# A different order of the first loads, and of the first matmuls, in a gated S5 and MLP kernel

## The chip, the core and the metric

The kernel runs on one core of a Trainium2 chip. The metric is the device time of one execution in microseconds (us). Before the change three runs took 214.64, 214.77 and 215.53 us, so the time before is 214.77 us, their median.

## What is computed

For 2048 tokens x of width 640 the kernel computes two branches and mixes them with a gate of one number per token:

```python
g = sigmoid((x * gate_w).sum(-1, keepdims=True))
# branch A: a diagonal complex recurrence of 640 states, and a skip
Bu = einsum("bld,pd->blp", x, B_bar)
h  = Lam_bar * h + Bu[:, t, :]            # for t in range(2048)
a  = 2.0 * einsum("blp,dp->bld", hseq, Cmat).real + x * Dskip
# branch B: a two-layer perceptron with 1728 hidden units
b  = gelu(x @ w1 + b1) @ w2 + b2
out = g * a + (1 - g) * b
```

All inputs and the output are bf16.

## The kernel before

**Tiles.** The tokens are cut into four chunks of 512, and a chunk into four token tiles of 128. The width 640 is five blocks of 128, counted by `kd`. A matmul needs x with its width on the partitions, so each chunk has a turned copy `xT[c]` of 128 partitions x 5 blocks x 512 tokens. The hidden width 1728 is thirteen blocks of 128 and a rest of 64, counted by `kf`. The first six blocks of w1 (768 columns) lie in five tiles `w1a[kd]`, one for each row strip of w1; in this text a strip is the 128 rows of one `kd`. The next four blocks are `w1b[kd]`, the rest is `w1c`.

**Main order.** After the start the kernel goes through the chunks: `ff1` (x times w1, with GELU on ScalarE, lines 274 to 321), `ssm` (x times B on TensorE, then the recurrence on VectorE), `fin_b` (times w2) and `fin_a` (times C, and the final mix). The order on TensorE, VectorE and ScalarE is the order in which the program is written (line 195 sets a manual schedule); the function `later` and its relatives place VectorE's work by estimated times. DMAs are issued by three engines: SyncE (SP), ScalarE (ACT) and GpSimd (POOL), each in program order.

**The first loads.** For chunk 0 the turned copy is made in two ways. Width blocks 0 and 1 of each token tile are loaded as they are (`load_x0`, lines 134 to 142, 64 KB for a tile) and turned by TensorE against an identity (`turn`, line 239); the result in PSUM is copied to `xT[0]` by VectorE for block 0 and by ScalarE for block 1 (`turned`, line 243). Width blocks 2 to 4 come by a transposing DMA, one for each half of the chunk (`load_turned`, lines 149 to 153). Lines 137 to 143 issue, on SyncE: token tile 0, strip 0 of `w1a`, token tile 3, strip 2; on ScalarE: token tile 1, strip 1, token tile 2. After that SyncE issues the two transposes and strips 4 and 3. A strip of `w1a` is 192 KB in rows of 1536 B. Behind its three loads ScalarE has a table load for its functions and a first `Exp` (line 147).

**The first matmuls.** Lines 236 and 237 fill the wait for the first data with nine matmuls on constants, whose results are not used. `turn_first(a, ...)` (line 251) turns both blocks of token tile `a`. Lines 357 to 369 then write the order out by hand: `part(kd, a)` is six matmuls of 128 columns, one for each of six `kf`, of strip `kd` with token tile `a`; `strip(kd, t0, t1, ...)` is the same with the tokens from t0 to t1. The six `kf` add up in six PSUM banks (`banks`), and with `pA` and one more bank for the turning all eight banks of PSUM are taken. After `part(1, 3)` come strip 2 in two halves (it needs the transposing DMAs), strip 4 and strip 3 (lines 376 to 393).

**A second chain in the start.** The matmul at line 370 turns a tile of small parameters. From it VectorE makes the arguments of the sine tables (lines 371 to 383), ScalarE loads the sine table and computes both tables (lines 382 and 384), then loads the GELU table and begins the GELUs of chunk 0 (line 282). Later ScalarE writes a bias into one bank (line 292), which the 20 matmuls of line 299 need.

Of the kernel before, what the change touches and what calls it, by code (L numbers as in the profile page):

```python
# [16 lines left out]
P = 128  # L17
T = 2048
D = 640
# [8 lines left out]
TPC = CH // P  # L28
H = TPC // 2
HT = H * P  # L30
# [11 lines left out]
def kernel(  # L42
# [19 lines left out]
    nc = tc.nc  # L62
# [12 lines left out]
    def bank(dtype=F32):  # L75
        return ps.tile([P, CH * 4 // (4 if dtype == F32 else 2)], dtype, name="bank")


    cut1 = FA * P
# [4 lines left out]
    w1a = [const.tile([P, cut1], BF16, name=f"w1a_{kd}") for kd in range(KD)]  # L84
# [37 lines left out]
        r0 = c * CH + a0 * P  # L122
        (queue or nc.sync).dma_start(out=xn[c][:, a0:a1, :], in_=x2d[r0:r0 + (a1 - a0) * P, :].rearrange("(a p) d -> p a d", p=P))

    def load_w1a(queue, kd):
        queue.dma_start(out=w1a[kd][:], in_=B_w1[kd * P:(kd + 1) * P, 0:cut1])

    def rows(queue, dst, v):
        queue.dma_start(out=dst, in_=v.rearrange("(j p) -> j p", p=P))
# [1 line left out]
    KA = 2  # L131
    xn[0] = xnp.tile([P, TPC, D], BF16, name="xn")

    def load_x0(queue, a0, a1, d0, d1):
        queue.dma_start(out=xn[0][:, a0:a1, d0:d1], in_=x2d[a0 * P:a1 * P, d0:d1].rearrange("(a p) d -> p a d", p=P))  # L135

    load_x0(nc.sync, 0, 1, 0, KA * P)
    load_x0(nc.scalar, 1, 2, 0, KA * P)
    load_w1a(nc.sync, 0)
    load_w1a(nc.scalar, 1)  # L140
    load_x0(nc.sync, 3, 4, 0, KA * P)
    load_x0(nc.scalar, 2, 3, 0, KA * P)
    load_w1a(nc.sync, 2)
    nc.vector.memset(prmA[:], 0.0)
    nc.vector.memset(prmB[:], 0.0)
    warm = const.tile([P, 1], F32, name="warm")
# [2 lines left out]
    def load_turned(a):  # L149
        nc.sync.dma_start_transpose(out=xT[0][:, KA:KD, a * P:(a + H) * P], in_=x2d[a * P:(a + H) * P, KA * P:D])  # L150

    load_turned(0)
    load_turned(H)
    load_w1a(nc.sync, 4)
    load_w1a(nc.sync, 3)
# [27 lines left out]
        nc.sync.dma_start(out=w2_sb[:, k0:k1, :], in_=B_w2[k0 * P:k1 * P, :].rearrange("(kf p) d -> p kf d", p=P))  # L183
    for h in range(2):
        nc.sync.dma_start(out=w2l[h * F_LAST:(h + 1) * F_LAST, :], in_=B_w2[(KF - 1) * P:F, :])
    load_x0(nc.sync, 0, H, KA * P, D)
    load_x0(nc.sync, H, TPC, KA * P, D)
    nc.sync.dma_start(out=b2bc[:], in_=B_b2.rearrange("(o d) -> o d", o=1).to_broadcast([P, D]))
    nc.sync.dma_start(out=Dbc[:], in_=A_Dskip.rearrange("(o d) -> o d", o=1).to_broadcast([P, D]))
    nc.sync.dma_start_transpose(out=xT[2][:], in_=x2d[2 * CH:3 * CH, :])  # L190
# [42 lines left out]
    nc.vector.tensor_copy(out=tf[:, NQ:NP], in_=tfi[:])  # L233
    ones = lambda n: nc.const_aps.tensor(1.0, [P, n], BF16)
    pA = bank()
    for n in (512, 512, 512, 512, 512, 128, 128, 128, 128):
        nc.tensor.matmul(pA[:, 0:n], lhsT=ones(P), rhs=ones(n), start=True, stop=True)

    def turn(p, col, a, kd):
        nc.tensor.matmul(p[:, col:col + P], lhsT=xn[0][:, a, kd * P:(kd + 1) * P], rhs=ident[:], start=True, stop=True,  # L240
                         skip_group_check=True)

    def turned(engine, p, col, a, k0, k1):
        dst = xT[0][:, k0:k1, a * P:(a + 1) * P]
        src = p[:, col:col + (k1 - k0) * P].rearrange("p (k t) -> p k t", t=P)
        if engine is nc.vector:
            nc.vector.tensor_copy(out=dst, in_=src)
        else:
            nc.scalar.activation(out=dst, in_=src, func=ACT.Identity)

    def turn_first(a, other, t=None):
        t = t or bank()
        turn(t, 0, a, 0)
        turned(nc.vector, t, 0, a, 0, 1)
        turn(other, a * P, a, 1)
        turned(nc.scalar, other, a * P, a, 1, 2)

    turn_first(0, pA)
    def col(name, dtype=F32, n=KS):
        return const.tile([P, n], dtype, name=name)  # L260
# [13 lines left out]
    def ff1_mm(p, c, kf, kd, t0=0, t1=CH, first=None, last=KD - 1):  # L274
        w, f0 = (w1a, 0) if kf < FA else (w1b, FA) if kf < FB else (w1c, FB)
        w = w[kd][:, (kf - f0) * P:(kf - f0 + 1) * P]
        nc.tensor.matmul(p[:, t0:t1], lhsT=w, rhs=xT[c][:, kd, t0:t1],  # L277
                         start=(kd == 0) if first is None else first, stop=(kd == last), skip_group_check=first is not None)
        pe(t1 - t0)
# [51 lines left out]
    def strip(kd, t0, t1, first, f0=0, f1=FA):  # L331
        for kf in range(f0, f1):
            ff1_mm(banks[kf], 0, kf, kd, t0, t1, first, 3)
# [20 lines left out]
    def part(kd, a):  # L354
        strip(kd, a * P, (a + 1) * P, kd == 0)

    turn_first(1, banks[FA - 1], banks[FA - 2])
    for _ in range(3):
        nc.tensor.matmul(banks[0][:, 0:P], lhsT=ones(P), rhs=ones(P), start=True, stop=True, skip_group_check=True)
    part(0, 0)  # L360
    part(0, 1)
    part(1, 0)
    turn_first(2, pA)
    part(1, 1)
    turn_first(3, pA)
    part(0, 2)
    part(1, 2)
# [367 lines left out]
```

## Time and profile before

The profiled execution has a span of 212.8 us, and its run took 214.58 us. TensorE's granted clock has a mean of 0.999 over the span.

| engine | busy us | share of the span | instructions |
|---|---|---|---|
| TensorE matmul (PE) | 208.9 | 98% | 1382 |
| TensorE weight load (PEld) | 125.0 | 59% | 1382 |
| VectorE (DVE) | 183.2 | 86% | 335 |
| ScalarE (ACT) | 102.0 | 48% | 184 |
| GpSimd (POOL) | 62.7 | 29% | 101 |

A row of a timeline gives the start in us, the duration from the first start to the last end, the engine, the line, the operation, what it writes and reads, the shape and the count; in brackets stands the idle time before it and what ended it. "SPq" and "ACTq" are the queues on which SyncE and ScalarE issue DMAs: such a row is the time that the issuing takes, not the transfer. A matmul's duration includes the time that it takes to drain; matmuls overlap, so the distance from start to start (the pitch) tells what one costs. A list of DMA issues gives the line, the queue, the count, the KB of each and the median us from issue to landing.

### The profile page before, as it was taken

What the parts mean: (1) busy time and instruction counts of PE and PEld (TensorE: products, weight loads), DVE (VectorE), ACT (ScalarE), POOL (GpSimd) and SP (SyncE); (2) the same over time, 40 slices, a digit from 0 to 9 for tenths busy, and PEclk for the clock granted to TensorE, in tenths of its full rate; (3) what the DMA queues carried; (4) which work ended last, traced back from release to release, by engine and by line L of the source; (5) the groups of instructions that cost most, each with busy time, mean ns of one, the idle gap of its engine ahead of it and who ended that gap; (6) DMA issues with size and microseconds to landing.
All of it is one profiled execution on the core that took longest, in us unless ns stands there. A gap on an engine that the chain in (4) does not pass through costs nothing.

```text
span 212.8 us, 3603 instructions
## 1 busy us (share of the span) xinstructions
PE 208.9 (98%) x1382; PEld 125.0 (59%) x1382; DVE 183.2 (86%) x335; ACT 102.0 (48%) x184; POOL 62.7 (29%) x101
## 2 busy tenths in 40 slices
PE   7999999999999999999999999999999999999994
PEld 4744444454576544774456777444457587676773
DVE  1589999999989999999999999999999999903153
ACT  3599856675858687103653210456682422205100
POOL 7044079764432462404235503146000000000000
PEclk9999999999999999999999999999999999999999
DMA  6999999995000000051000005100000000100011
GB/s 182 249 221 219 218 212 366 217 217 154 3 0 0 3 0 0 12 186 65 0 0 3 0 17 171 62 0 0 0 5 14 0 3 31 62 34 0 0 63 65
DMA packets 33314, 16.24 MB, mean 76 GB/s; under 512 B 24720, under 2 KB 33296, under 8 KB 33296
## 3 DMA queue, kind: packets, MB, share of 16 engines
q1 hardware_dynamic: 32560, 15.64, 29.7%
q10 hardware_dynamic: 576, 0.36, 0.5%
q8 instruction: 11, 0.18, 0.3%
q14 instruction: 7, 0.06, 0.1%
q0 software_dynamic: 160, 0.01, 0.1%
HBM read 7.48 MB, written 2.62 MB: 47 GB/s over the span
## 4 chain that ended last, share of the span: by engine, by line
PE 97%; DMA 2%; SPq 0%; DVE 0%; issue 0%
PE bank L602 27%; PE bank L277 27%; PE bank L661 20%; PE bank L545 20%; DMA w1a<-in_B_w_dram 2%; PE bank L618 1%; PE bank L299 1%; SPq L135 0%; PE bank L240 0%; DVE ot L666 0%; PE bank L387 0%; PE bank L370 0%
## 5 line engine op out<-in xcount | busy, mean ns | idle before, releaser
L602 PE MATMUL bank<-w_sb,gel 128*128 128x384 bf16 (+1 forms) x416 | 57.9, 299 | 0.0
L602 PEld LDWEIGHTS <-gel 128*128 128x128 bf16 x416 | 40.3, 98 | 17.0 <-issue 0.8
L548 ACT ACTIVATE bu<-bank 128x512 bf16<-128x512 f32 x40 | 23.6, 605 | 37.5 <-PE bank L545 37.5
L282 ACT ACTIVATE gel<-bank,colB 128x512 bf16<-128x512 f32 x52 | 34.0, 695 | 10.8 <-PE bank L277 10.6
L661 PEld LDWEIGHTS <-hs 128*128 128x128 bf16 x330 | 31.7, 98 | 11.6
L509 POOL TENSOR_SCALAR e<-g,cq 128x2 f32<-128x2 bf16 x15 | 18.3, 1222 | 64.3 <-DVE g L502 64.3
L502 DVE TENSOR_TENSOR_SCAN g<-r_c,carry,v 128x512 bf16<-128x512 f32 x30 | 37.2, 1271 | 0.0
L610 ACT ACTIVATE gb<-bank,gcol 128x384 f32<-128x384 f32 (+1 forms) x32 | 15.1, 526 | 33.7 <-PE bank L618 16.8
L277 PE MATMUL bank<-xT,w1a 128*128 128x512 bf16 (+2 forms) x162 | 27.0, 324 | 0.3 <-DMA w1a<-in_B_w_dram 0.3
L661 PE MATMUL bank<-CT_re,hs 128*128 128x320 bf16 (+2 forms) x165 | 27.1, 295 | 0.0
L661 PE MATMUL bank<-CT_im,hs 128*128 128x320 bf16 (+2 forms) x165 | 27.1, 295 | 0.0
L666 DVE SCALAR_TENSOR_TENSOR ot<-bank,gcol,gb 128x320 bf16<-128x320 f32 (+2 forms) x33 | 17.4, 533 | 9.7 <-PE bank L661 9.5
L545 PE MATMUL bank<-xT,BT_re 128*128 128x512 bf16 x100 | 24.8, 379 | 0.0
L545 PE MATMUL bank<-xT,BT_im 128*128 128x512 bf16 x100 | 24.8, 379 | 0.0
L277 PEld LDWEIGHTS <-w1a 128*128 128x128 bf16 x162 | 13.8, 98 | 12.2 <-DMA w1a<-in_B_w_dram 0.6
L576 DVE TENSOR_TENSOR bank<-xn,Dbc 128x320 f32<-128x320 bf16 (+2 forms) x33 | 14.6, 484 | 7.0 <-ACT gb L610 7.0
L277 PE MATMUL bank<-xT,w1b 128*128 128x512 bf16 x80 | 17.9, 379 | 0.0
L545 PEld LDWEIGHTS <-BT_im 128*128 128x128 bf16 x100 | 9.8, 98 | 11.8
L511 POOL TENSOR_TENSOR carry<-e,e 128x1 f32<-128x1 f32 x30 | 15.8, 546 | 1.2
L545 PEld LDWEIGHTS <-BT_re 128*128 128x128 bf16 x100 | 9.7, 98 | 11.0
L483 DVE TENSOR_TENSOR v<-wa,wb 128x512 bf16<-128x512 bf16 x40 | 15.2, 422 | 0.6
L591 ACT ACTIVATE bank<-b2bc 128x384 f32<-128x384 bf16 (+1 forms) x24 | 11.7, 529 | 7.2 <-DVE ot L666 7.2
(110 smaller groups left out, 216.2 us busy)
## 6 DMA issues: line engine op xcount, KB each, us to landing
out_dram<-ot SPq DMA_DIRECT2D x15, 160.0 KB, 1.8
w_sb<-in_B_w_dram SPq DMA_DIRECT2D x2, 640.0 KB, 6.8
xn<-in_A_x_dram SPq DMA_DIRECT2D x2, 640.0 KB, 4.3
w_sb<-in_B_w_dram SPq DMA_DIRECT2D x1, 800.0 KB, 9.6
w1a<-in_B_w_dram SPq DMA_DIRECT2D x4, 192.0 KB, 3.3
w1b<-in_B_w_dram SPq DMA_DIRECT2D x5, 128.0 KB, 3.3
xn<-in_A_x_dram SPq DMA_DIRECT2D x4, 160.0 KB, 3.0
xn<-in_A_x_dram SPq DMA_DIRECT2D x2, 192.0 KB, 8.3
```

The source lines that it names most:

```text
L277: nc.tensor.matmul(p[:, t0:t1], lhsT=w, rhs=xT[c][:, kd, t0:t1], start=(kd == 0) if first is None else first, stop=(kd == last), skip_grou ...
L282: nc.scalar.activation(out=gel[c][:, kf, :], in_=p[:, :], func=ACT.Gelu_apprx_tanh, bias=b1_c[:, kf:kf + 1])
L483: nc.vector.tensor_tensor(out=o, in0=a, in1=b, op=op)
L502: nc.vector.tensor_tensor_scan(s["g"][:, ri, :], r_c[:, ks:ks + 1].to_broadcast([P, CH]), s["v"][:, ri, :], init, ALU.mult, ALU.add)
L509: nc.gpsimd.tensor_scalar(out=t[:], in0=g[:, :, CH - 1], scalar1=f[:, ks:ks + 1], scalar2=None, op0=ALU.mult)
L511: nc.gpsimd.tensor_tensor(out=carry[:, ri, ks:ks + 1], in0=m[0][:, ri:ri + 1], in1=m[1][:, 1 - ri:2 - ri], op=op)
L545: nc.tensor.matmul(p[:], lhsT=BT[ks >= KSA][:, kd, (ks % KSA if ks < KSA else ks - KSA) * P:][:, 0:P], rhs=xT[c][:, kd, :], start=(kd == 0 ...
L548: nc.scalar.activation(out=bu[:, ri, :], in_=p[:], func=ACT.Identity)
L602: nc.tensor.matmul(p[:, col:col + d1 - d0], lhsT=gel[c][:, kf, a * P:(a + 1) * P], rhs=w2_sb[:, kf, d0:d1], start=False, stop=False, skip_ ...
L610: nc.scalar.activation(out=gbs[ti][:, d0:d1], in_=p[:, col:col + d1 - d0], func=ACT.Identity, scale=gcol[:, 1, ti:ti + 1])
L661: nc.tensor.matmul(p[:, 0:d1 - d0], lhsT=hs[c][:, j, lo:lo + P], rhs=CT[:, j % KS, d0:d1], start=False, stop=(j == 2 * KS - 1), skip_group ...
L666: nc.vector.scalar_tensor_tensor(out=ot[:, d0:d1], in0=p[:, 0:d1 - d0], scalar=gcol[:, 0, ti:ti + 1], in1=gbs[ti][:, d0:d1], op0=ALU.mult, ...
```

## The change

The edits, all in the start but for one load:

- ScalarE's queue now issues strip 0 of `w1a` in two halves of 384 columns (96 KB, rows of 768 B): the first half, token tile 1, the second half, token tile 2. That is four DMAs where there were three.
- SyncE's queue issues token tile 0, then strip 1, token tile 3, the first transpose, strip 2, the second transpose, strips 4 and 3.
- A later load on SyncE, width blocks 2 to 4 of token tiles 0 to 3, becomes one DMA in place of two.
- Two of the nine matmuls on constants are left out.
- For token tile 0, block 1 is copied from PSUM by VectorE instead of ScalarE.
- `part(1, 0)` and `part(1, 1)`, which stood around the turning of token tile 2, become one `strip(1, 0, 256)` of six matmuls of 256 columns behind that turning.

```diff
-    def load_w1a(queue, kd):
-        queue.dma_start(out=w1a[kd][:], in_=B_w1[kd * P:(kd + 1) * P, 0:cut1])
+    def load_w1a(queue, kd, f0=0, f1=cut1):
+        queue.dma_start(out=w1a[kd][:, f0:f1], in_=B_w1[kd * P:(kd + 1) * P, f0:f1])
...
     load_x0(nc.sync, 0, 1, 0, KA * P)
+    load_w1a(nc.scalar, 0, 0, cut1 // 2)
+    load_w1a(nc.sync, 1)
     load_x0(nc.scalar, 1, 2, 0, KA * P)
-    load_w1a(nc.sync, 0)
-    load_w1a(nc.scalar, 1)
     load_x0(nc.sync, 3, 4, 0, KA * P)
+    load_w1a(nc.scalar, 0, cut1 // 2)
     load_x0(nc.scalar, 2, 3, 0, KA * P)
-    load_w1a(nc.sync, 2)
...
     load_turned(0)
+    load_w1a(nc.sync, 2)
     load_turned(H)
...
-    load_x0(nc.sync, 0, H, KA * P, D)
-    load_x0(nc.sync, H, TPC, KA * P, D)
+    load_x0(nc.sync, 0, TPC, KA * P, D)
...
-    for n in (512, 512, 512, 512, 512, 128, 128, 128, 128):
+    for n in (512, 512, 512, 512, 512, 128, 128):
...
-        turned(nc.scalar, other, a * P, a, 1, 2)
+        turned(nc.scalar if a else nc.vector, other, a * P, a, 1, 2)
...
     part(0, 0)
     part(0, 1)
-    part(1, 0)
     turn_first(2, pA)
-    part(1, 1)
+    strip(1, 0, HT, False)
     turn_first(3, pA)
```

## The prediction

> **What bounds the kernel now.** I read the busy table first (in the section above): TensorE works 98% of the span. Then the chain of waits in order of time, because only what lies on it can move the end. Its first pieces, with start and duration in us:
>
> ```profile
> 0.72 0.40 SPq L135
> 1.12 0.06 issue
> 1.18 3.30 DMA w1a<-in_B_w_dram
> 4.48 0.05 issue
> 4.52 1.18 PE bank L277 x18
> ```
>
> From 4.52 us to 209.99 us every piece of the chain is TensorE work, so the kernel is one wait for strip 0 of w1, then TensorE without a pause, then a short tail. The change can gain only by starting that work earlier or by taking idle time out of it. So next the timeline of the start:
>
> ```profile
> 3.27 0.63 PE L240 MATMUL bank<-ident,xn 128*128 128x128 bf16 x4
> 3.70 0.49 PE L359 MATMUL bank<-const-bfloat16-1.0 128*128 128x128 bf16 x3
> ...
> 4.52 1.18 PE L277 MATMUL bank<-xT,w1a 128*128 128x128 bf16 x18 [0.34 <-DMA w1a<-in_B_w_dram]
> ...
> 5.54 0.28 PE L240 MATMUL bank<-ident,xn 128*128 128x128 bf16 x2
> ...
> 5.65 0.50 PE L277 MATMUL bank<-xT,w1a 128*128 128x128 bf16 x6
> 5.80 0.29 DVE L247 CAST xT<-bank 128x128 bf16<-128x128 f32 x1 [1.67 <-PE bank L240]
> ...
> 6.14 0.27 PE L240 MATMUL bank<-ident,xn 128*128 128x128 bf16 x2
> ```
>
> Two idle stretches show. The first ends at 4.52 with strip 0. The second is small: the six matmuls from 5.65 have a pitch of (0.50 - 0.22)/5 = 0.056 us (one alone lasts 0.22 in the group's own list), so the last starts at 5.93 and the next could start at 5.99. It starts at 6.14, 0.05 after VectorE's copy of token tile 2 ends (5.80 + 0.29). The turn of tile 3 needs the PSUM bank that this copy empties, so 0.15 us are lost.
>
> When data came is read from the list of DMA issues, asked in narrow windows. The four in flight between 1.4 and 2.0 us:
>
> ```profile
> w1a<-in_B_w_dram ACTq DMA_DIRECT2D x1, 192.0 KB, 3.6
> w1a<-in_B_w_dram SPq DMA_DIRECT2D x1, 192.0 KB, 3.3
> xn<-in_A_x_dram SPq DMA_DIRECT2D x1, 64.0 KB, 3.3
> xn<-in_A_x_dram ACTq DMA_DIRECT2D x1, 64.0 KB, 3.5
> ```
>
> With the issue times of the timeline (1.15, 1.18, 1.64, 1.65) they land at 4.75, 4.48, 4.94 and 5.15. Other windows of the same list give: tiles 0 and 1 at 2.8 and 2.9, strip 2 at 5.8, the transposes at 7.1 and 7.7 (2.59 + 4.5, 3.96 + 3.7), strip 4 at 8.6 (5.28 + 3.3).
>
> Last, the ScalarE rows and the weight load that waits for them:
>
> ```profile
> 12.19 4.73 ACT L282 ACTIVATE gel<-bank,colB 128x512 bf16<-128x512 f32 x8
> ...
> 18.56 0.47 ACT L292 ACTIVATE bank<-b1x 128x260 f32<-128x260 bf16 x1
> 18.87 1.34 ACT L282 ACTIVATE gel<-bank,colB 128x512 bf16<-128x512 f32 x2
> ...
> 19.08 0.66 PEld L299 LDWEIGHTS <-xT 128*128 128x128 bf16 x20 [0.32 <-ACT bank L292]
> ```
>
> ScalarE works without a gap from 10.3 us on, and its row L292 ends at 19.03, just as TensorE needs it (its next matmul starts at 19.09, with no idle time). TensorE can gain over this place only if the ScalarE chain moves too. It does: that chain begins with the matmul L370 at 7.26 (then VectorE, the sine tables, the GELU table load at 10.89), which is in TensorE's order behind the part that moves.
>
> **What the Trainium skill says.** "DMA: Bandwidth & Descriptors", section "Queues, rings and completion order": SP and ACT own one ring each on the same 16 engines, and an engine goes round among the rings. The trace agrees: the two strips, one on each queue, land 0.27 us apart, and the mean DMA share is 1.09 from 3.25 to 4.50 us. So a load that moves to the other queue gains place, not bandwidth. "TensorE: Matmul & The Clock Gate", section "What's actually happening": TensorE starts at half clock and is released after a busy window of about 3.4 us; the window runs free of the kernel. The trace agrees: the turns at 3.27 have a pitch of (0.63 - 0.31)/3 = 0.107 us, the matmuls from 4.52 one of (1.18 - 0.22)/17 = 0.056 us. The release lies between, over 3 us after the first matmul (0.76).
>
> **The change, part by part.**
>
> *Loads.* I put each landing on a curve "KB asked for up to here, time of landing" from the kernel before: 128 KB at 2.9, 512 KB at 4.6 (mean of 4.48 and 4.75), 640 KB at 5.05, 832 KB at 5.8. This assumes that the two rings share bytes evenly. After the change ScalarE's ring holds 96 (strip 0a), 64 (tile 1), 96 (strip 0b), 64 (tile 2), and SyncE's 64 (tile 0), 192 (strip 1), 64 (tile 3), then the first transpose. A load ends when its own ring has given its KB and the other as many. Strip 0a: 192 KB at most, 3.2. Tile 1: 320 KB, 3.75. Strip 0b and strip 1: 512 KB, 4.6. Tiles 2 and 3: 640 KB, 5.05 to 5.15. No row shows these landings in the new order; I keep 4.8 and 5.6 as the ends for tile 2 (the first two rivals) and take 5.15.
>
> *Start.* Two matmuls on constants fewer: 0.21 us at a pitch of 0.107, hidden before and after by the wait for loads. Tile 0 is turned at 3.06, tile 1 at 3.8 when it lands. VectorE now makes three copies where it made two (0.29 each; tile 0's lie in the wait), and the third follows the turn by 0.36 (3.27 to 3.63 before): 4.16 to 4.45. ScalarE issues a fourth DMA (0.45), so table load (1.28) and Exp (0.20) end near 4.1 instead of 3.63; its one copy (tile 1) runs from 4.27 to 4.55, hidden by strip 0b. The first three matmuls of strip 0 can run near 4.3 with the first half. The other three wait for the second half at 4.6, so the fourth runs at 4.65, where it ran at 4.52 + 3 x 0.056 = 4.69. **The half strips bring some 0.05 us**, because the second half is needed 0.17 us after the first.
>
> *Middle.* Eight more matmuls (the other two of part(0, 0), six of part(0, 1)) end at 5.15, about when tile 2 lands; its turn starts at about 5.18, before at 5.54. But six matmuls that stood ahead of it (6 x 0.056 = 0.335) now stand behind it, as half of the six with 256 columns. Those cost 6 x 0.109 = 0.655 (the pitch is my estimate, twice 0.056 less a small fixed part), 0.02 less than twelve small ones. They lie between the turns of tiles 2 and 3, so the copy of tile 2 (ready 0.65 after its turn) is done in time and the loss of 0.15 goes. **Gain up to strip 2: 5.54 - 5.18 - 0.335 + 0.15 + 0.02 = 0.2 us.** Strip 2 begins at 7.42 instead of 7.62 (7.28 + 6 x 0.056).
>
> *Does it last?* The first transpose has 192 KB less ahead of it: near 6.6 instead of 7.1. Strip 2 now comes between the transposes, estimated 7.1, needed at 7.42. The second transpose has the same KB ahead as before: 7.7, needed at 8.07. Strip 4 has the same place, and four issues of 0.45 and two of 1.3 ahead of it on SyncE as before: 8.6, needed at 8.93 - 0.2 = 8.73. All hold, strip 4 with 0.13 us to spare: **the gain is capped at 0.33 us there.** SyncE's new order adds no wait that blocks: strip 2's issue reuses the semaphore of strip 0a (landed by 3.2, issue at 3.45), the second transpose's that of tile 0. The single load of tiles 0 to 3 saves one SyncE issue; its data are wanted by `seed(0)` only near 80 us, so it counts nothing.
>
> *Sum.* 0.2 us off the profiled span of 212.8 us, which is the run of 214.58; the other runs were 214.64, 214.77 and 215.53. From the median: 214.77 - 0.2 = 214.6 us. No difference under 0.5% (1.07 us) can be told from none here; faster means under 213.70, slower over 215.84.
>
> **Rivals.** (1) *Capped gain.* ScalarE's ring runs ahead and tile 1, strip 0b and tile 2 land 0.3 us earlier; the turn of tile 2 starts at 4.9, the gain would be 0.48 and strip 4 caps it at 0.33: 214.4. For it: DMA share of only 0.86 from 2.50 to 3.25 us, which smaller first loads may fill. Against: 1.09 right after. (2) *Tile 2 late.* It is now fourth on ScalarE's queue, issued at 2.1 instead of 1.65, and the transpose runs beside it. If it lands as much later as it is issued, 5.6, then 5.54 - 5.65 - 0.165 = -0.27: 215.0. Against: at 2.1 its ring still has 2 us of data ahead. (3) *The clock, the slower side.* Before, matmuls run from 0.76 to 4.19 without a gap; after, TensorE idles some 0.5 us between the turns of tiles 0 and 1 and again before strip 0b. If the window around 3 us then no longer counts as busy, the release comes one window later: 4.0 + 3.4 = 7.4, and the work from 4.65 to 7.4 runs at half speed. That loses 2.75/2 = 1.4 us: 214.6 + 1.4 = 216.0. It makes the kernel slower than before as soon as the release falls later than 4.65 + 2 x 0.2 = 5.05 us, and slower by more than the bound from 7.2 us on. Against: the gaps are under a fifth of a window. (4) *Nothing arrives*, because ScalarE's chain holds L299: 214.8; against it stands that L370 moves with the rest.
>
> **How the numbers follow.** Forecast 0.50, capped gain 0.20, tile 2 late 0.18, clock 0.08, nothing arrives 0.04. Low end: if strip 4 also comes earlier, 0.48 off the fastest run, 214.64, is 214.16, and less again by the spread of 0.13 between the fastest and the median: 214.0. High end: tile 2 late, 215.0, and half a microsecond for a run like the 215.53: 215.5. Outside lie the clock case and the tails. Faster by over 0.5%: 0.03, since no mechanism above gives 1.07 us. Slower: 0.09, the clock case and a little. Within: 0.88.
>
> **What would show it.** Tile 1's turn near 3.8 and a gap ahead of it; strip 0's fourth matmul waiting for a DMA until about 4.65; tile 2's turn at about 5.2; no idle time ahead of tile 3's turn; strip 2 near 7.4; L299 near 18.9. Wrong, if the pitch is still 0.107 us after 4.7, if strip 2, or strip 4 ends a wait of over 0.2 us, or if L299 stays at 19.09.

## The result, and the profile after

The changed kernel is slower. Six runs took 215.98, 216.94, 217.28, 217.63, 217.69 and 218.55 us, median 217.45; six runs of the kernel before on the same chip have a median of 214.74. The ratio is 1.0114, with a 95% interval from 1.0075 to 1.0153. The runs also scatter over 2.6 us, where those of before scatter over 0.9. The profiled execution is the fastest of the six: its span is 213.9 us. The spans of all six are 213.9, 214.8, 215.2, 215.5, 215.6 and 215.9.

This is the chain of waits of the changed kernel, its first pieces in order of time (start, duration in us, what). The lines to hold beside it are the first five of the prediction.

```profile
0.72 0.41 ACTq L126
1.15 0.46 ACTq L135
1.65 0.45 ACTq L126
2.13 4.31 DMA xn<-in_A_x_dram
6.49 0.28 PE bank L240 x2
```

The end was set by strip 0 on SyncE's queue before (landing at 4.48). Now it is set by token tile 2, the fourth load on ScalarE's queue: issued at 2.13, landed at 6.44. From there on TensorE works to the end, as before. The timeline of TensorE in the same execution shows the two waits that TensorE has instead of one:

```profile
3.06 0.42 PE L240 MATMUL bank<-ident,xn 128*128 128x128 bf16 x2
4.32 0.28 PE L240 MATMUL bank<-ident,xn 128*128 128x128 bf16 x2 [0.83 <-DMA xn<-in_A_x_dram]
...
4.61 0.33 PE L277 MATMUL bank<-xT,w1a 128*128 128x128 bf16 x3
5.70 0.68 PE L277 MATMUL bank<-xT,w1a 128*128 128x128 bf16 x9 [0.76 <-DMA w1a<-in_B_w_dram]
6.49 0.28 PE L240 MATMUL bank<-ident,xn 128*128 128x128 bf16 x2
6.61 0.82 PE L277 MATMUL bank<-xT,w1a 128*128 128x256 bf16 x6
7.26 0.27 PE L240 MATMUL bank<-ident,xn 128*128 128x128 bf16 x2
...
8.38 0.17 PE L369 MATMUL bank<-ident,prmA 128*128 128x10 bf16 x1
```

TensorE is idle for 0.83 us until token tile 1 is there and for 0.76 us until the second half of strip 0 is there; the turn of tile 2 then starts at 6.49, where it started at 5.54. The last row, the turning of the parameter tile, is a good milestone, since in both kernels TensorE works from there to the end with no wait over 0.06 us. It stands at 8.38; in the kernel before it is this row, at 7.26:

```profile
7.26 0.17 PE L370 MATMUL bank<-ident,prmA 128*128 128x10 bf16 x1
```

These 1.12 us are the whole difference of the two profiled spans (213.9 and 212.8). So **in its fastest run the change loses 1.1 us, all of it in the first eight microseconds, and all of it by data that come late.** The other five runs lose more; the experiments show where.

The list of DMA issues of the changed kernel, for the loads issued from 1.4 to 3 us (two narrow windows):

```profile
w1a<-in_B_w_dram SPq DMA_DIRECT2D x1, 192.0 KB, 2.9
w1a<-in_B_w_dram ACTq DMA_DIRECT2D x1, 96.0 KB, 4.0
xn<-in_A_x_dram ACTq DMA_DIRECT2D x1, 64.0 KB, 3.1
xn<-in_A_x_dram SPq DMA_DIRECT2D x1, 64.0 KB, 2.9
```

```profile
xn<-in_A_x_dram ACTq DMA_DIRECT2D x1, 64.0 KB, 4.3
```

On SyncE's queue strip 1 lands at 4.07 and tile 3 at 4.54, earlier than the loads in these places did. On ScalarE's queue tile 1 lands at 4.27, the second half of strip 0 (96 KB, 4.0 us after its issue) at 5.65 and tile 2 at 6.44. The table of stretches says what the transfers did meanwhile. A row has the stretch, its length, busy time and count of TensorE, weight loads, VectorE, ScalarE and GpSimd, then the granted clock, the mean share of the DMA engines and GB/s. First the changed kernel, then the kernel before:

```profile
4.00:4.50 0.50, 0.18 (x4) 0.19 (x5) 0.00 (x0) 0.11 (x1) 0.50 (x6) 1.00 0.73 134
4.50:5.00 0.50, 0.44 (x8) 0.27 (x5) 0.29 (x1) 0.28 (x1) 0.14 (x5) 1.00 1.06 156
```

```profile
4.00:4.50 0.50, 0.19 (x3) 0.00 (x0) 0.13 (x1) 0.22 (x2) 0.50 (x6) 1.00 1.17 372
4.50:5.00 0.50, 0.48 (x9) 0.48 (x10) 0.00 (x0) 0.00 (x0) 0.13 (x4) 1.00 1.03 307
```

In this microsecond the kernel before moves (372 + 307) x 0.5 = 340 thousand bytes, the changed one 145 thousand. That does not mean that the same loads ran more slowly. The packet records of the two traces, which list the start, length and size of every piece that a queue moves, say what was left to move. By 4.00 us the two queues of the changed kernel had moved 318 KB (SyncE) and 253 KB (ScalarE), 571 KB in all; those of the kernel before 281 and 252, 533 KB. From 4.00 to 5.00 the kernel before moves 288 KB of loads and 38 KB of its first transpose, whose packets begin at 4.65. In the changed kernel they begin at 3.98: strip 2 stands behind the transpose now, and the microsecond holds 61 KB of loads and 78 KB of transpose.

The same records part a load's data from its landing. A landing is the last of 16 updates of the load's semaphore, the counter on which its reader waits. In the changed kernel the last packet of strip 0's second half ended at 4.15 and 14 of its 16 updates had come by 4.71; the last two came at 5.60 and 5.65. From 4.90 to 5.46 no load of any queue sent an update. Tile 2's last packet ended at 5.31, its last update came at 6.44; in the kernel before these two times are 4.52 and 5.18.

One figure stays unexplained. The device time of a run exceeds its span by about 1.78 us in the kernel before, 1.94 at most in all its runs. In the changed kernel the excess is 1.73 to 2.08 in four runs, and 2.89 and 2.95 in the other two (217.69 and 218.55 us). It was seen in other kernels with idle stretches too (up to 2.9), and no view of the trace reaches it.

### The profile page after: what moved, and what is told of

Read it like the earlier page. It is cut to its first block, busy times and chain, and to the rows that moved or that the text cites. A ratio compares the mean times of both kernels' runs of the same rounds, so it can differ in the third digit from the quotient of the medians.

```text
span 213.9 us, 3576 instructions
## 1 busy us (share of the span) xinstructions
PE 208.1 (97%) x1363; PEld 124.4 (58%) x1374; DVE 183.4 (86%) x336; ACT 101.8 (48%) x183; POOL 62.4 (29%) x101
## 3 DMA queue, kind: packets, MB, share of 16 engines
HBM read 7.48 MB, written 2.62 MB: 47 GB/s over the span
## 4 chain that ended last, share of the span: by engine, by line
PE 95%; DMA 2%; ACTq 1%; issue 0%; DVE 0%
PE bank L601 27%; PE bank L277 26%; PE bank L660 20%; PE bank L544 20%; DMA xn<-in_A_x_dram 2%; PE bank L617 1%; PE bank L299 1%; ACTq L126 0%; ACTq L135 0%; PE bank L240 0%; DVE ot L665 0%; PE bank L386 0%; PE bank L369 0%
## 5 line engine op out<-in xcount | busy, mean ns | idle before, releaser
(110 smaller groups left out, 214.6 us busy)
```

## The experiments

Four theories were on the table. *Loads*: token tiles 1 and 2 and the second half of strip 0 come late because of their places on ScalarE's queue. *Clock*: the idle stretches let a window of TensorE's activity fail, so that full clock comes a window later. *Transposes*: the first transpose, now ahead of strip 2, holds the other loads up. *Compute*: the edits on TensorE and VectorE cost something themselves. Times are medians, beside the kernel before of the same batch, with the ratio and its 95% interval. TensorE's clock is read from the pitch of the matmuls. Of the 18 traces 13 also hold a record of the stretch at full clock, and its beginning is called the release here (4.01 us in the kernel before, 3.90 in the changed kernel's first trace).

### The transposes

In **e1** the changed kernel gets strip 2 back ahead of the first transpose; in **e2** the kernel before gets only this part of the change.

```diff
 (e1, from the changed kernel; e2 does the reverse to the kernel before)
-    load_turned(0)
     load_w1a(nc.sync, 2)
+    load_turned(0)
     load_turned(H)
```

> The changed kernel with one thing undone: strip 2 stands ahead of the first transpose on SyncE's queue again. Theory T (the first transpose, running beside ScalarE's ring, crowds out the second half of strip 0 and tile 2): both land near 4.6 and 5.2 us instead of 5.65 and 6.44, strip 2 begins near 7.4 to 7.7 instead of 8.74, and the time is 214.4 to 215.0 us. Theory O (the order on ScalarE's own ring is at fault: four loads, tile 1 behind a half strip): the landings stay within 0.3 us of the changed kernel's and the time stays near 217.4 us. Theory C (TensorE's clock is released late in most executions because TensorE idles twice): the idle stretch ahead of tile 1's turn stays, 3.3 to 4.3 us, so about half of the excess over the profiled 1.1 us stays, 216 us.

> The kernel before with only one thing of the change: the first transpose stands ahead of strip 2 on SyncE's queue. Theory T: ScalarE's tile 2 is the last load of its ring here too, and transpose packets run beside it; it lands at 5.3 to 6.2 us instead of 5.15, and the time rises by 0.1 to 0.8 us, to 214.9 to 215.6. Theory O: nothing changes, 214.7 to 214.8 us. Theory C: no idle time is added ahead of 4 us, so 214.7 us as well.

e1: 216.58 against 214.89 us, ratio 1.0075 (1.0044 to 1.0106); spans 213.6 to 216.6. Token tile 2 landed at 6.08, the second half of strip 0 at 5.51, nearly as late as in the changed kernel (two more traces of it, e11 and e12 below, have tile 2 at 6.21 and 6.02), so the 4.6 and 5.2 of theory T did not come. Nor did the 217.4 of theory O: the median is 0.87 us lower than that of the changed kernel, but the two intervals overlap. e2: 215.02 against 214.89, ratio 0.9999 (0.9986 to 1.0011). The place of the first transpose alone costs no time that can be measured in the kernel before. In the profile of e2, however, tile 2 lands at 5.72, within what theory T expected; in the five profiles with the loads of before (before, e4, e7, e9, e10) it lands from 5.04 to 5.54. TensorE did not wait for it, since strip 0 was there only at 4.74 and the turn of tile 2 began at 5.80.

Both runs move the first transpose behind or ahead of strip 2; none takes it away. Its packets begin at 4.83 in e1 and at 3.91 in e2, beside tile 2's last packets in both. So what these two runs show is that this one swap is not the main loss, not that the transposes leave ScalarE's loads alone.

In **e5** e1 got the filling of the next experiment too.

> The changed kernel with both edits at once: strip 2 ahead of the first transpose again, and the matmuls on constants in TensorE's two idle stretches, so that the clock's scatter is out of the comparison. With the gaps filled alone the time was 215.81 us, 0.92 over the kernel before. Theory T (transposes crowd ScalarE's loads): what moving the transpose gave in the profile, strip 2 at 8.38 instead of 8.74 us, shows in the times too, 215.3 to 215.6 us. If the whole of the loads' cost were the transpose's, 214.7 to 214.9. Theory O (the order on ScalarE's own ring): most of the 0.92 stays, 215.4 to 215.8 us.

e5: 215.96 against 214.86, ratio 1.0041 (1.0027 to 1.0055), next to the 1.0040 of e3, its counterpart with the transpose ahead (theory O had 215.4 to 215.8, theory T less). In its profile the release is at 6.64 us, so that the four filling matmuls ran at half clock and themselves held up strip 0; the comparison is blurred by that, and says only that no large effect of the transpose hides there.

### Filling the idle stretches

**e3** is the changed kernel with matmuls on constants in both stretches: nine of 128 columns ahead of the turn of tile 1, four of 512 columns between the third and the fourth matmul of strip 0. **e4** goes the other way: the kernel before, without its matmuls on constants (lines 237 and 359), whose results are not used. Its loads stay as they are.

```diff
 (e3, from the changed kernel)
+    fill(banks[0], P, 9)
...
-    part(0, 0)
+    strip(0, 0, P, True, 0, 3)
+    fill(banks[3], CH, 4)
+    strip(0, 0, P, True, 3, FA)
 (e4, from the kernel before)
-    for n in (512, 512, 512, 512, 512, 128, 128, 128, 128):
+    for n in ():
...
-    for _ in range(3):
+    for _ in range(0):
```

> The changed kernel, with matmuls on constants put into TensorE's two idle stretches: nine of 128 columns ahead of tile 1's turn, four of 512 columns between the third and fourth matmul of strip 0 with tile 0. The loads are those of the changed kernel. Theory C: the clock is released near 4 us in every execution, the scatter shrinks to some 0.5 us and the median falls from 217.45 to about 216.0 us, what the loads alone cost. Theories T and O: the loads set the time and their scatter is the scatter of the times, 217.0 to 217.8 us.

> The kernel before without its nine and three matmuls on constants, which prices a late release of TensorE's clock by itself; loads and all other work unchanged. Matmuls then begin near 2.9 us with idle time up to 4.5. If the release needs a mostly busy window of about 3.4 us, it falls between 6.5 and 10 us, and the time rises by 1.0 to 2.7 us, to 215.8 to 217.5, with a scatter of that order. If the clock is no cause of such differences, 214.7 us.

e3: 215.81 against 214.89, ratio 1.0040 (1.0026 to 1.0054), the seven runs within 0.8 us. Matmuls that compute nothing take 1.6 us off the median and the scatter of 2.6 us away. They are not free either, as the timeline of TensorE in e3 shows:

```profile
5.13 1.03 PE L359 MATMUL bank<-const-bfloat16-1.0 128*128 128x512 bf16 x4
...
6.50 0.28 PE L240 MATMUL bank<-ident,xn 128*128 128x128 bf16 x2
```

The second half of strip 0 had landed at 5.53 and tile 2 at 6.18; without the filling the turn could have begun at 6.23, so the filling costs about 0.3 us.

e4: 216.32, ratio 1.0057 (1.0037 to 1.0078). Its loads land as before (strip 0 at 4.29, tile 2 at 5.11), but its matmuls keep a pitch of 0.107 us until 8.78, and the milestone (line 370) stands at 9.00 instead of 7.26:

```profile
4.33 2.10 PE L277 MATMUL bank<-xT,w1a 128*128 128x128 bf16 x18 [0.85 <-DMA w1a<-in_B_w_dram]
...
9.00 0.17 PE L370 MATMUL bank<-ident,prmA 128*128 128x10 bf16 x1
```

So idle time before 4.5 us alone can make this kernel slower by more than a microsecond.

### Two more traces of the changed kernel

The first profile was the fastest of six runs. **e11** and **e12** are the changed kernel again, to see a slower one.

> The changed kernel once more, for a trace of a longer execution than the 213.9 us of its first profile. Theory C: if the span is over 214.5 us, the landings of tile 1, strip 0's second half and tile 2 are within 0.4 us of those of the first profile (4.3, 5.65, 6.44) and the matmuls keep a pitch of 0.107 us until well after 6.5 us. Theory T or O alone: the pitch is 0.056 us from 4.5 us on and the loads land later by as much as the span is longer.

> The same kernel, a second look, with the same expectation as the first: over 214.5 us of span the late release (theory C) or later landings (T, O) must show; near 213.9 us neither does.

e11 took 215.62 us (span 213.7) and resembles the first profile: release at 4.10, tile 2 landed at 6.21. e12 took 216.84 us (span 215.1). Its timeline of TensorE:

```profile
4.26 0.39 PE L240 MATMUL bank<-ident,xn 128*128 128x128 bf16 x2 [0.78 <-DMA xn<-in_A_x_dram]
...
6.34 0.42 PE L240 MATMUL bank<-ident,xn 128*128 128x128 bf16 x2
6.55 1.49 PE L277 MATMUL bank<-xT,w1a 128*128 128x256 bf16 x6
...
8.05 1.59 PE L277 MATMUL bank<-xT,w1a 128*128 128x128 bf16 x18
9.48 0.17 PE L369 MATMUL bank<-ident,prmA 128*128 128x10 bf16 x1
```

Two matmuls of the turn take 0.42 us where the first profile has 0.28, six of 256 columns take 1.49 where it has 0.82: TensorE is at half clock until about 8.9. Data did not come later here (tile 2 landed at 6.02, its turn begins 0.15 us earlier than in the first profile). Yet the milestone stands at 9.48 instead of 8.38, and the span is 1.2 us longer. This is the clock's part of the loss, seen directly. The granted clock in the table of stretches doesn't show it (it says 1.00 all through these microseconds, in both executions); the pitch of the matmuls does.

### The order on ScalarE's queue

**e6** is the changed kernel with tile 1 first on ScalarE's queue: tile 1, the two halves of strip 0, tile 2. **e14** leaves strip 0 whole, first on that queue: strip 0, tile 1, tile 2. **e8** is e14 with the filling of e3.

```diff
 (e6, from the changed kernel)
+    load_x0(nc.scalar, 1, 2, 0, KA * P)
     load_w1a(nc.scalar, 0, 0, cut1 // 2)
...
-    load_x0(nc.scalar, 1, 2, 0, KA * P)
 (e14, from the changed kernel)
-    load_w1a(nc.scalar, 0, 0, cut1 // 2)
+    load_w1a(nc.scalar, 0)
...
-    load_w1a(nc.scalar, 0, cut1 // 2)
```

> The changed kernel with token tile 1 first on ScalarE's queue, then the two halves of strip 0 and tile 2; nothing filled. Theory O with C (tile 1 is late because it stands second on ScalarE's ring, and the idle stretch this makes ahead of its turn delays the clock): tile 1 lands near 2.9 us instead of 4.3, the idle stretch from 3.3 to 4.3 goes, the three matmuls on constants follow at once, and the median falls by 0.3 to 1.2 us from 217.45, to 216.2 to 217.1; strip 0's second half and tile 2 stay late (5.3 to 6.4 us). If only the second stretch matters for the clock, the median stays at 217.2 to 217.7.

> The kernel with the gaps filled, but strip 0 as one load of 192 KB, first on ScalarE's queue, then tile 1 and tile 2; the rest of the changed order stays. If cutting strip 0 (a fourth load, its second half behind tile 1) is what makes it late, all of strip 0 lands by 4.5 us instead of 5.5, strip 2 of w1 begins at 8.2 to 8.5 us instead of 8.75, and the time falls from 215.81 to 215.3 to 215.6. If the place of tile 2 (last on ScalarE's ring, beside the transpose) sets the time whatever stands ahead of it, tile 2 lands at 6.0 to 6.4 us as with the halves and the time is 215.6 to 216.0.

> The changed kernel with strip 0 as one load, first on ScalarE's queue, without any filling matmuls: three loads on ScalarE's queue as before, the rest of the change as it is (two constants fewer, first transpose ahead of strip 2). Theory P: tile 2 is third and lands at 5.1 to 5.6 us, not at 6.0 to 6.4; the shortest spans fall to 212.8 to 213.2 us from the changed kernel's 213.7, though tile 1 (second) still lands near 4.3 us. Theory C: the idle stretch ahead of tile 1 stays, so a group of spans some 2 us longer stays as well and the median is 215 to 216.5 us. Theory B: with the same KB on the ring nothing moves, and the shortest span is 213.7 us.

e6: 215.54 against 214.86, ratio 1.0044 (1.0024 to 1.0064). Its 22 runs fall into two groups, 15 with spans from 213.1 to 213.7 and 7 from 214.8 to 215.5. With tile 1 back in first place TensorE works without a gap until about 4.0, and the late group becomes the smaller one (the median fell below the expected 216.2 to 217.1); the second half of strip 0 and tile 2 still come at 5.54 and 6.07. e14: 217.18 against 214.80, ratio 1.0088 (1.0054 to 1.0123), spans mostly from 214.8 to 215.3; its profile has half clock until about 9.5. Undoing the halves doesn't bring the time back: tile 1, in second place, still lands at 4.37, and TensorE idles for 0.70 us ahead of its turn, as theory C expected (its 215 to 216.5 for the median was too low). Theory P was near, but missed: tile 2 in third place lands at 5.74 (5.1 to 5.6 was expected), and the shortest span is 213.4 (212.8 to 213.2). e8: 216.28, ratio 1.0060 (1.0042 to 1.0077). Strip 0 as one load lands at 3.44 and tile 2 at 5.29, both earlier than expected, yet the time is above the 215.3 to 215.6 that were to follow: in its profile the release is at 5.79 and the filling itself held the work up, so its time separates nothing.

### The compute edits alone

**e7** has the loads of before and the changed compute: VectorE's third copy, the merged `strip(1, 0, HT)`, seven constants. **e9** is the same with all nine constants. **e10** is e7 again, run once for a trace.

```diff
 (e7, from the kernel before; e9 leaves the first edit out)
-    for n in (512, 512, 512, 512, 512, 128, 128, 128, 128):
+    for n in (512, 512, 512, 512, 512, 128, 128):
...
-        turned(nc.scalar, other, a * P, a, 1, 2)
+        turned(nc.scalar if a else nc.vector, other, a * P, a, 1, 2)
...
-    part(1, 0)
     turn_first(2, pA)
-    part(1, 1)
+    strip(1, 0, HT, False)
```

> The kernel before, all its loads as they were, with only the change's edits on TensorE and VectorE: seven matmuls on constants instead of nine, block 1 of tile 0 copied by VectorE, strip 1 for tiles 0 and 1 as six matmuls of 256 columns behind the turn of tile 2. By the prediction's own sum the idle 0.15 us ahead of tile 3's turn goes, tile 2 is turned at about 5.2 us, and the time is 0.1 to 0.2 us less: 214.6 to 214.8 beside 214.75 to 214.9 for the kernel before. If these edits are a cause of the loss (two constants fewer, clock later), 215.0 us or more.

> The kernel before with the edits on TensorE and VectorE but with all nine matmuls on constants: the compute-only kernel with its two left-out constants back. That kernel's spans fell into two groups, eight at 212.6 to 213.4 us and six at 214.6 to 215.4. Theory C (TensorE's idle time ahead of strip 0, some 0.2 us longer with two constants fewer, makes a busy window fail): the upper group goes, all spans lie at 212.5 to 213.6, and the median time is 214.5 to 214.8 us, at or just under the kernel before. If the constants are no cause, two groups remain and the median is near 216 us.

> The compute-only kernel once more, for a trace. If its span falls in the upper group (214.6 us or more), theory C says that matmuls of 128 columns keep a pitch of 0.107 us beyond 7 us, with the landings as before; if the pitch is 0.056 us from 4.5 us on, something else makes the group. In the lower group (213.4 or less) the release lies before 6.9 us.

e7: 216.03 against 214.86, ratio 1.0041 (1.0011 to 1.0071), in two groups: 8 runs with spans from 212.6 to 213.4, 6 from 214.6 to 215.4. The profiled run is of the lower group, and so is e10 (214.35 us, span 212.6). The timeline of TensorE in e7:

```profile
4.41 0.84 PE L277 MATMUL bank<-xT,w1a 128*128 128x128 bf16 x12 [0.50 <-DMA w1a<-in_B_w_dram]
5.17 0.28 PE L240 MATMUL bank<-ident,xn 128*128 128x128 bf16 x2
5.29 0.82 PE L277 MATMUL bank<-xT,w1a 128*128 128x256 bf16 x6
...
7.06 0.17 PE L369 MATMUL bank<-ident,prmA 128*128 128x10 bf16 x1
```

The milestone stands at 7.06, 0.20 us earlier than before, and the span is 0.2 us shorter. About half of that is luck: strip 0 landed at 4.37 here and at 4.48 before. From the first matmul of strip 0 to the milestone the kernel before takes 2.74 us, e7 2.65 and the profile of e9 2.62, so the edits themselves show some 0.1 us of the 0.2 that the prediction worked out. The second group, 2 us later, is what two missing constants do. With them back, e9 took **214.73 us against 215.09 for the kernel before**, ratio 0.9978 (0.9965 to 0.9991): 22 runs in one group, spans from 212.7 to 213.7. It is faster than both kernels, if only by 0.2%. The kernel before is not quite free of the late group either: 4 of its 160 runs in all batches have spans from 214.8 to 215.3, 2 of them among the 27 beside e9. That the upper group of e7 is a late clock wasn't seen in a trace of such a run; it is argued from e9 and from the distance, which is near that of e4 (1.8 in the profile).

### One more load ahead of token tile 2

In the runs so far the loads ahead of tile 2 differ in place, KB and rows at once. Three kernels change only these, in the kernel before: one more load on ScalarE's queue ahead of tile 2, into a tile that nothing reads. **e13** loads 16 KB in 128 rows of 128 B, **e15** 16 KB in 16 rows of 1024 B, **e16** 192 KB in 128 rows of 1536 B.

```diff
 (e13, from the kernel before; e15: 16 rows of 512 columns; e16: P rows of 768 columns)
+    junk = const.tile([P, 64], BF16, name="junk")
+    nc.scalar.dma_start(out=junk[:], in_=B_w1[0:P, 0:64])
     load_x0(nc.scalar, 2, 3, 0, KA * P)
```

> The kernel before with one small extra load on ScalarE's queue, ahead of tile 2: 16 KB of w1 into a tile that nothing reads. (By the reuse of its semaphore SyncE's first transpose is held some 0.3 us, which has 0.5 us to spare.) Theory P (a landing is set by the place on the ring: each load from the third on adds some 0.5 to 0.9 us whatever its KB): tile 2, now fourth, lands at 5.9 to 6.4 us instead of 5.0 to 5.5, the turn of tile 2 waits, and the median rises by 0.3 to 0.8 us over the kernel before. Theory B (bytes set the landing, as in the prediction's curve): 16 KB move it by under 0.1 us, and the time stays within 0.1 us of the kernel before.

> Kernel before plus one more load on ScalarE's queue ahead of token tile 2, again 16 KB, but as 16 rows of 1024 B in place of 128 rows of 128 B (the data are not used). With 128 rows tile 2 landed at 6.03 us and the time was 215.74. If a load counts by its number of rows (packets), the 16 rows are nearly free: tile 2 lands between 5.2 and 5.6 (5.15 before, plus at most the later issue of 0.48), the span grows by 0 to 0.3 us, the time is near 215.0. If a load counts by its place on the queue whatever it is, tile 2 lands near 6.0 and the time is near 215.7. If it counts by its KB, as in the run with 128 rows: near 6.0 too.

> Kernel before plus one more load on ScalarE's queue ahead of token tile 2, 192 KB as 128 rows of 1536 B, twelve times the KB of the run with 128 rows of 128 B (the data are not used). If a load counts by its number of rows, or by its place, tile 2 lands near 6.0 to 6.2 us, as with 16 KB, and the time is near 215.8. If it counts by its KB, 176 KB more at the 0.3 KB/ns of this stage are 0.5 to 0.6 us more: tile 2 lands near 6.6, the time is near 216.3.

e13: 215.74 against 214.80, ratio 1.0044 (1.0029 to 1.0059). e15: 215.71 against 214.89, ratio 1.0041 (1.0030 to 1.0052). e16: 215.87, ratio 1.0041 (1.0029 to 1.0053). Three loads that differ twelvefold in KB and eightfold in rows cost the same. From the chain of waits of e13:

```profile
2.13 3.90 DMA xn<-in_A_x_dram
...
6.08 0.28 PE bank L242 x2
```

Tile 2 now sets the end, as in the changed kernel. The list of DMA issues of e15 has the load that pushed it back:

```profile
xn<-in_A_x_dram ACTq DMA_DIRECT2D x1, 64.0 KB, 4.0
...
junk<-in_B_w_dram ACTq DMA_DIRECT2D x1, 16.0 KB, 3.6
```

In fourth place tile 2 lands at 6.03, 6.17 and 6.25 us, in third place (before) at 5.18. Its issue comes 0.48 later, its landing 0.85 to 1.07. KB and rows are ruled out as the main price. Its last packet ends at 5.39, 5.36 and 5.63 (before: 4.52), so it is the data that come later here. They now run beside the first transpose, whose packets begin at 4.67, 4.66 and 5.21; before, tile 2 was through ahead of them (4.65). How much of the 0.85 to 1.07 is the later issue, how much the transpose and how much the place on the queue, these runs don't say. In these kernels the milestone and the last VectorE work move by 0.5 to 0.9 us (e13: the milestone from 7.26 to 7.80; in e16 the release is only at 6.72, which adds to it); a further 0.4 us of their longer spans lies after the last work, and that isn't explained.

Put together, landings on ScalarE's queue in ten of the profiled runs, in us, with the KB of the load in brackets:

| kernel | first | second | third | fourth |
|---|---|---|---|---|
| before | 2.94 (64) | 4.74 (192) | 5.18 (64) | |
| e16 | 3.06 (64) | 4.64 (192) | 5.46 (192) | 6.25 (64) |
| e15 | 2.96 (64) | 5.03 (192) | 5.22 (16) | 6.17 (64) |
| e13 | 3.03 (64) | 4.83 (192) | 5.25 (16) | 6.03 (64) |
| e2 | 2.89 (64) | 4.96 (192) | 5.72 (64) | |
| e14 | 3.49 (192) | 4.37 (64) | 5.74 (64) | |
| e8 | 3.44 (192) | 4.36 (64) | 5.29 (64) | |
| e5 | 3.08 (96) | 4.21 (64) | 4.83 (96) | 6.05 (64) |
| e6 | 3.01 (64) | 4.34 (96) | 5.54 (96) | 6.07 (64) |
| the changed kernel | 3.12 (96) | 4.27 (64) | 5.65 (96) | 6.44 (64) |

Read down a column, the KB vary up to twelvefold and the landing by at most 0.9 us (1.0 over all 18 profiles; tile 2 in third place, with no change of the loads, varies by 0.5). Read along a row, each place further costs 0.2 to 2.1 us, about 1 in the mean, of which 0.43 to 0.50 is the later issue.

## Why the prediction was wrong

The time, 217.45 us, lies outside the range of 214.0 to 215.5 and on the other side of no change.

**The step that failed is *Loads*:** the landings were put on a curve of KB, which "assumes that the two rings share bytes evenly", and a load was taken to land when its KB are through. It gave tile 1 at 3.75, strip 0b at 4.6 and tile 2 at 5.15; measured were 4.27, 5.65 and 6.44. The KB themselves were not behind: 571 KB were through by 4.00, more than in the kernel before, and strip 0b's last packet ended at 4.15. Two terms are missing from the curve. It could not hold them, since in the kernel before ScalarE's loads were through (4.52) before the first transpose began (4.65). One is the stretch beside the transpose: tile 2's last packets took until 5.31. The other is the time from a load's last packet to its landing: 1.50 us for strip 0b and 1.13 for tile 2, where tile 2 had 0.66 before.

In terms of places, the change moves tile 1 from first to second place, the data of the fourth matmul from second place on SyncE to third on ScalarE, and tile 2 from third to fourth. Each is late by about one place (1.33, 1.17 and 1.26 us), and with tile 2 begins the chain of the fastest run. The extra loads of e13, e15 and e16 show that one load more ahead of tile 2 does this by itself, whatever its KB. The rival *tile 2 late* named the right load with too small a price: it delayed the landing by the later issue alone (5.6), where e13 to e16 measure twice that; "the transpose runs beside it" stands in it without a price. The section "Queues, rings and completion order" of the Trainium skill's page "DMA: Bandwidth & Descriptors" says that an engine takes whole packets in turn from the rings, not bytes; that speaks against even bytes, and the trace agrees: by 4.00 us the changed kernel's queues had moved nearly the same number of rows, 381 on SyncE and 383 on ScalarE, but 318 KB and 253 KB. A count of rows alone doesn't explain the landings either, as e15 shows.

**The second failure is the weight of the clock**, the rival *(3)*, given 0.08. Its mechanism was right, and its 216.0 is of the size of what e12 shows (216.84, where late data add to it). "The gaps are under a fifth of a window" was said against it. With late loads the two gaps were 0.83 + 0.76 = 1.6 us, nearly half of one. Even with the loads of before, 6 of 14 runs had the second group (e7). So also the two constants, priced as "0.21 us at a pitch of 0.107, hidden", weren't hidden: they kept TensorE busy, and taking them out had a price that no idle time shows. The Trainium skill's page "TensorE: Matmul & The Clock Gate", section "What's actually happening", has the window at 3413 ns and free of the kernel, with a transition that varies by 500 ns either way. The traces agree on the window (last section), not on the 500 ns: the release was seen from 3.40 to 6.72 us in the 13 traces that record it, nearly a whole window wide, and at about 8.9 (e12, by the pitch) when one had failed.

How much idle time makes a window fail can be estimated. Lay windows of 3.413 us end to end so that one ends at the release, and add up TensorE's idle time in each, the time ahead of the first matmul included. The window that ended in the release held 0.78 us at most (e1, from -0.01 to 3.40 us, nearly all of it ahead of the first matmul). Windows that did not bring full clock held 0.87 (e16), 0.95 (e5) and, with the release read from the pitch, 0.89 (e12), 0.76 (e14) and 1.78 (e4); all others held over 1.4. So the limit lies near 0.8 of 3.4 us; this is an estimate from these 18 traces. By it the gap of 0.67 us in e9's profile passes, and the same gap with two constants (0.21 us) fewer fails. In the five profiles with the loads of before strip 0 landed from 4.23 to 4.85, so e7 would pass in some runs and fail in others. That fits its two groups, but no trace of its late group exists.

**How the median adds up.** The median of the changed spans is 215.35, that of before about 214.74 - 1.78 = 212.96: 2.4 us. Late data account for 0.9 to 1.1 of it (the spans of 213.7 and 213.9 with an early clock, against 212.8). The other 1.3 to 1.5 are put down to the late clock: e12 shows it at 1.2, and with the gaps filled (e3) the median falls by 1.6, but the longer ones of the six runs have no trace. The remaining 0.3 of the 2.71 us between the device medians lie outside the span and stay open.

**What was right.** *Middle*: from the turn of tile 2 to the first matmul of strip 2 the prediction has 7.42 - 5.18 = 2.24 us, and the trace 8.74 - 6.49 = 2.25; no idle time is left ahead of tile 3's turn. That these edits gain was measured by e9, with nine constants. VectorE's third copy, which is part of e9, has no cost that shows there, and SyncE's order has none in the time of e2. *Does it last?* wasn't put to the test: strip 2 landed at 7.48 and strip 4 at 8.68 (7.1 and 8.6 were predicted), ahead of a TensorE that was late itself. ScalarE's chain did not hold the line 299 up: its matmuls, at 19.26 in the chain before, moved with TensorE to 20.38.

**What stays open.** Why a place costs about 1 us whatever the load: no kernel issued a load later in the same place, and none took the transposes out, so the place itself, the later issue that comes with it and the transpose that a late load runs beside are not told apart. Why the last two updates of strip 0b came 0.9 us after the others. And the time outside the span.

## What to carry to other kernels

At the start of a kernel like this one, count the places on each queue and what runs beside them, not only the KB: whatever is needed first must stand first, and cutting a load in two so that a part of it comes sooner puts everything behind it one place further back (in e13, e15 and e16 one place cost tile 2 0.85 to 1.07 us). A load's data and its landing are two times: where a landing seems late, read the packets too. Matmuls on constants that fill a wait are part of the schedule as long as the clock isn't released: before taking two of them out, or opening a gap, price the half-clock window that may follow (1 to 2 us here), not the idle time. Take several executions where a profile may show only the lucky case, and read the pitch of the matmuls to see which case it is.

## What the runs showed of the hardware that was not expected

- An extra load of 16 KB whose data nothing reads cost 0.8 to 0.9 us of 215 (e13, e15); one of 192 KB in the same place cost 0.98 (e16). Some 0.4 us of each lies after the last work of the kernel.
- Strip 0's second half was moved by 4.15 us, but landed at 5.65: two of its 16 updates came 0.9 us after the other 14 (4.71), and from 4.90 to 5.46 no load of any queue sent one. The packets of the first transpose had begun at 3.98. That the transpose holds the updates back is not shown.
- The stretch at full clock that the traces record is 208.213 or 211.626 us long, whichever the kernel. Both are whole numbers of windows (61 and 62 times 3.413 us), and they differ by one. So the clock goes on and off on a grid of that step, and the releases from 3.40 to 6.72 us say that a kernel can begin anywhere on it.
- The twelve matmuls on constants, whose results nobody reads, are worth 1.4 us to the kernel before (e4), and two of them decide between a ratio of 1.0041 and one of 0.9978 (e7 and e9).
